# First pass of a fused attention and feed-forward kernel: low weight halves from GpSimd to VectorE, kept bits from GpSimd to ScalarE

## The chip, the cores and the metric

The kernel runs on one core of a Trainium2 chip. The metric is the device time of one execution in microseconds (us), lower is better. Three executions of the kernel before took 726.46, 723.76 and 724.49 us, median 724.49 us. The execution that the profiler recorded took 722.97 us, of which 721.2 us are the span from the first to the last instruction.

## The reference, cut to what matters

```
attn = softmax(causal(q k^T / sqrt(64))) v          # 4 batches, 12 heads, 448 tokens, head size 64
x    = attn as (1792, 768)
xn   = x / sqrt(mean(x^2) + 1e-6) * rms_g
g    = xn @ w_gate                                   # (768, 1536)
out  = (g * sigmoid(g) * (xn @ w_val)) @ w_out       # (1536, 768)
```

q, k, v and rms_g come as 32-bit floats. The three weight matrices come as 64-bit floats and are turned into 32-bit floats on the chip.

## The kernel before, in words

**Splitting.** TensorE multiplies in a rounded 32-bit format (F32R). To keep accuracy each operand is split in two parts, a rounded high part and the rest: `w_h = round(w)`, `w_l = w - w_h` for a weight, `xh`, `xl` for the input and `hh`, `hl` for the hidden layer. Each product is three matmuls: L450 takes `w_h` and `xh`, L451 `w_h` and `xl`, L452 `w_l` and `xh`.

**Passes.** The tokens are worked in three groups: two of 512 and one of 768. The first pass of the feed-forward layer (`s` = 0 to 35, 36 weight tiles of 128x768) works on the first group while the attention of the second group runs between its matmuls; the second pass (`s` = 36 to 71) works on the second group beside the attention of the third; the last part (L600) works on the third group with a fast matrix product. Only the first pass meets the 64-bit weights: it writes each converted tile back to DRAM (`w32`), and the later parts read it from there.

**One weight tile in the first pass.** It is loaded as pairs of 32-bit words (`in_w`, 768 KB, into one of three buffers `w64`). Then:

- `L387`, ScalarE: the high word, read as a 32-bit float, times a power of two into `w_c`.
- `L388`, GpSimd: the high word times zero, so that only its sign is left.
- the kept bits: the top three bits of the low word are put beside that sign. For most tiles this is `L392`, VectorE (shift and or). For the tiles for which `bytes_` holds it is `L390`: the top byte of the low word, times 1/32 less 31/64, is rounded to a 16-bit integer in place. In the text these are the byte tiles. Before, they are the even tiles from 6 on, and L390 is GpSimd's.
- `L394`, VectorE: `w_c` shifted by three, or that word. This ends the use of the `w64` buffer; the load of the tile three later waits for it.
- `L396`: the store to `w32`.
- `L404`, ScalarE: `w_h`. Then `w_l`, on VectorE (`L406`) or on GpSimd (`pool_op`, `L105`).

**What sets the order.** The schedule is manual: the instructions stand on each engine in the order in which the Python code issues them, and every engine works its own queue in that order. Time is counted in ticks, three to a weight tile. `post(d, f)` issues `f` `d` ticks later; the table `T` holds the delays. Tile `s` is converted from five tiles ahead of its matmuls: L387 at once, L388 one tick later, the kept bits four ticks later (`c2`), L394 five ticks later (`c3`) or, for byte tiles, eight (`c38`). `split_w` issues L404 seven ticks ahead of the matmuls and `w_l` two ticks behind it (`wl`; 7 or 5 ticks for the first four tiles). Where two `L394` fall on one tick, they stand next to each other.

**Who empties the banks.** A finished bank of PSUM is read by VectorE: `L467` (`gr`, gate tile) or `L477` (`t_sb`, value tile), in the last tiles `L461`. There are two banks of the name `m_ps`, so the tile after next waits for that read. ScalarE computes the tanh (`L468`), `hh` (`L478`), the exponentials (`L206`) and copies transposed attention weights from PSUM (`L257`, `pt`) for the matmuls `L277`.

All DMAs are issued by SyncE (SP), one queue, in program order.

Of the kernel before, what the change touches and what calls it, by code (L numbers as in the profile page):

```python
# [16 lines left out]
ALU = mybir.AluOpType  # L17
AF = mybir.ActivationFunctionType
# [9 lines left out]
NF = DFF // P  # L28
NU = 2 * NF + 2 * KD
# [11 lines left out]
        for g in range(NG) for c in range(NP)}  # L41
# [2 lines left out]


T = dict(c0=0, c1=1, c2=4, c20=12, c3=5, c30=13, c38=8, c26=6, c36=7, c5=7, c50=16, c56=9, c58=10, exp=1, exp0=3, gt=1, hh=1, hl=4, ws=5, ld2=7,
         ld=4, ld1=11, lv=5, norm0=7, norm1=2, r0=1, r1=5, so=3, wl=2, wl0=7, wl2=5, xl=2, xl0=9)
LOAD = (4, 12, 24, 36, 48, 60, 74, 86)
CONVERT = (20, 32, 44, 56, 62, 93)
SPLIT = (33, 45, 57, 70)  # L50
# [14 lines left out]
def attention_ffn(ctx: ExitStack, tc: tile.TileContext, qk0, qk1, qk2, v, v2, w, g, out, out2):  # L65
# [7 lines left out]
    nc = tc.nc  # L73
# [27 lines left out]
    def f32(ap):  # L101
        return ap.bitcast(F32)

    def pool_op(out_, a, op, b):
        nc.gpsimd.tensor_tensor(out_, a, b, op=op)  # L105
# [27 lines left out]
    def post(delay, fn):  # L133
        if delay <= 0:
            fn()
        else:
            later.setdefault(now[0] + delay, []).append(fn)
# [7 lines left out]
    xr, xh, xl, acc, xq = {}, {}, {}, {}, {}  # L145
# [224 lines left out]
    def convert_ops(s):  # L370
        if s >= NU:
            return []
        raw_w = wt[s]
        t = wr_p.tile([P, DM], F32, tag="w", name="w_c")
        wt[s] = t
        ti, lo, hi = t.bitcast(I32), raw_w[:, :, 0], raw_w[:, :, 1]
        hf_ = raw_w.bitcast(F32)[:, :, 1]
        bytes_ = s > 5 and s % 2 == 0
        if bytes_:
            flat = raw_w.rearrange("p c t -> p (c t)")  # L380
            low = flat.bitcast(I16).rearrange("p (c t) -> p c t", t=4)[:, :, 2]
            top = flat.bitcast(U8).rearrange("p (c t) -> p c t", t=8)[:, :, 3]
        at2, at3, at5 = [T[n] for n in ("c20 c30 c50" if s < 5 else "c26 c36 c56" if s == 5 else
                                        "c2 c38 c58" if bytes_ else "c2 c3 c5").split()]

        return [
            (T["c0"], lambda: nc.scalar.mul(t, hf_, 2.0 ** -112)),  # L387
            (T["c1"], lambda: nc.gpsimd.tensor_scalar(  # L388
                hf_, hf_, 0.0, 1.0, op0=ALU.mult, op1=ALU.mult)),
            (at2, (lambda: nc.gpsimd.tensor_scalar(  # L390
                low, top, 1.0 / 32, -31.0 / 64, op0=ALU.mult, op1=ALU.add)) if bytes_ else
             (lambda: nc.vector.scalar_tensor_tensor(  # L392
                 out=hi, in0=lo, scalar=29, in1=hi, op0=ALU.logical_shift_right, op1=ALU.bitwise_or))),
            (at3, lambda: nc.vector.scalar_tensor_tensor(  # L394
                out=ti, in0=ti, scalar=3, in1=hi, op0=ALU.logical_shift_left, op1=ALU.bitwise_or)),
            (at5, lambda: nc.sync.dma_start(out=w32[s], in_=t)),  # L396
        ]

    def split_w(s):
        if s < 2 * NU:  # L400
            t = wt[s]
            h = ws_p.tile([P, DM], F32R, tag="wh", name="w_h")
            l = ws_p.tile([P, DM], F32R, tag="wl", name="w_l")
            nc.scalar.copy(h, t)  # L404
            if s in (1, 3, 5) or s % 2 == 0 and 4 != s < NU or s > NU + 2 * NF and s % 2:
                post(T[("wl0", "wl0", "wl2", "wl2")[s] if s < 4 else "wl"], lambda: nc.vector.tensor_tensor(l, t, f32(h), op=ALU.subtract))  # L406
            else:
                post(T["wl"], lambda: pool_op(l, t, ALU.subtract, f32(h)))
            wt[s] = tuple(a.rearrange("p (k m) -> p k m", m=P) for a in (h, l))
            u = s - NU  # L410
            if 0 <= u < 2 * NF:
                pair[u % 2] = t
                if u % 2:
                    post(T["ws"], lambda v=u // 2, t0=pair[0], t1=t: quad_sums(v, t0, t1))
# [4 lines left out]
    def quad_sums(v, t0, t1):  # L419

        a11, a12, a21, a22 = t0[:, : HX], t0[:, HX:], t1[:, : HX], t1[:, HX:]
        todo = [(a22, a21, a22, ALU.add), (a21, a11, a21, ALU.subtract),
                (a11, a22, a11, ALU.subtract), (a12, a12, a11, ALU.subtract)]
        for d, (o, x, y, op) in enumerate(todo):
            post(2 * d, lambda o=o, x=x, y=y, op=op: nc.vector.tensor_tensor(o, x, y, op=op))

        def store():
            for d, t in ((wy[v][:, : HX], a11), (wy[v][:, HX:], a22), (wz[v][:, : HX], a21), (wz[v][:, HX:], a12)):
                nc.sync.dma_start(out=d, in_=t)

        post(8, store)
# [383 lines left out]
    with tc.manual_schedule():  # L815
# [28 lines left out]
        for fs, at_ in ((load_w, LOAD), (lambda n: convert(n), CONVERT), (split_w, SPLIT)):  # L844
            for n, t_ in enumerate(at_):
                at_tick(t_, lambda fs=fs, n=n: fs(n))
# [13 lines left out]
        def convert(s):  # L860
            for d, op in convert_ops(s):
                post(d, op)
# [13 lines left out]
        for s in range(2 * NU):  # L876
# [15 lines left out]
            for k0 in (0, 2, 4):  # L892
# [9 lines left out]
                if k0 == (0 if s < 3 else 4) and s + 3 >= len(SPLIT):  # L902
                    split_w(s + 3)
# [129 lines left out]
```

## Time and profile before

| | before |
|---|---|
| median of 3 executions | 724.49 us |
| the profiled execution | 722.97 us |
| its span | 721.2 us |
| TensorE matmul (PE) busy | 683.3 us, 95% |
| VectorE (DVE) busy | 531.7 us, 74% |
| GpSimd (POOL) busy | 393.7 us, 55% |
| ScalarE (ACT) busy | 371.9 us, 52% |
| DMA bytes | 138.80 MB, mean 192 GB/s |

The shares are means over parts that differ: the attention of the first group alone, the first pass, the second pass, and the last part. The rows further below are read by stretches of the span. PEclk, or the granted clock, is the share of TensorE's full clock (2.4 GHz) that the chip granted in a stretch; its other level is half of it. In a row of operations the last part, behind the bar, is the time the engine sat idle just before these instructions and what ended it.

### The profile page before, as it was taken

What the parts mean: (1) busy time and instruction counts of PE and PEld (TensorE: products, weight loads), DVE (VectorE), ACT (ScalarE), POOL (GpSimd) and SP (SyncE); (2) the same over time, 40 slices, a digit from 0 to 9 for tenths busy, and PEclk for the clock granted to TensorE, in tenths of its full rate; (3) what the DMA queues carried; (4) which work ended last, traced back from release to release, by engine and by line L of the source; (5) the groups of instructions that cost most, each with busy time, mean ns of one, the idle gap of its engine ahead of it and who ended that gap; (6) DMA issues with size and microseconds to landing.
All of it is one profiled execution on the core that took longest, in us unless ns stands there. A gap on an engine that the chain in (4) does not pass through costs nothing. (4 is left out here: it accounts for less than half of the span.)

```text
span 721.2 us, 11890 instructions
## 1 busy us (share of the span) xinstructions
PE 683.3 (95%) x4108; PEld 555.8 (77%) x4108; DVE 531.7 (74%) x1017; ACT 371.9 (52%) x832; POOL 393.7 (55%) x324
## 2 busy tenths in 40 slices
PE   8879789988799999999999999999999999999998
PEld 6556567766566667777777777788899999999997
DVE  4997968778667546777768787739567678769993
ACT  6964566855577644534635534433534243355551
POOL 4995498465446763475667656565345354422220
PEclk9999899999799999999999999999999999999999
DMA  8662675845566854657575764533575665643541
GB/s 266 228 233 70 211 261 201 276 167 192 174 223 206 291 196 141 209 185 258 186 265 176 242 204 150 181 105 118 193 232 180 226 220 196 232 137 103 154 143 65
DMA packets 71355, 138.80 MB, mean 192 GB/s; under 512 B 7744, under 2 KB 39232, under 8 KB 71296
## 3 DMA queue, kind: packets, MB, share of 16 engines
q1 hardware_dynamic: 71296, 138.05, 58.1%
q8 instruction: 32, 0.52, 0.3%
q14 instruction: 27, 0.22, 0.1%
HBM read 104.21 MB, written 33.82 MB: 191 GB/s over the span
## 5 line engine op out<-in xcount | busy, mean ns | idle before, releaser
L211 POOL TENSOR_SCALAR sp<-sp,rs 128x384 f32<-128x384 f32 (+3 forms) x132 | 92.2, 716 | 90.9 <-DVE rs L215 76.3
L450 PE MATMUL m_ps<-xh,w_h 128*128 128x512 f32 x276 | 120.6, 437 | 8.9 <-DVE t_sb L477 4.7
L452 PE MATMUL m_ps<-xh,w_l 128*128 128x512 f32 x276 | 111.2, 403 | 2.1 <-POOL w_l L105 2.1
L451 PE MATMUL m_ps<-xl,w_h 128*128 128x512 f32 x276 | 110.6, 401 | 0.0
L206 ACT ACTIVATE sp<-sp,nm 128x384 f32<-128x384 f32 (+3 forms) x168 | 87.2, 523 | 39.7 <-DVE nm L203 39.7
L105 POOL TENSOR_TENSOR a_l<-w_q,a_h 128x768 fp32r<-128x768 f32 x24 | 48.1, 2003 | 65.9 <-ACT a_h L491 65.7
L277 PEld LDWEIGHTS a_ps<-pt,v_r 128*64 128x64 f32 (+1 forms) x864 | 43.8, 138 | 45.3 <-ACT pt L257 14.6
L277 PE MATMUL a_ps<-pt,v_r 128*64 128x128 f32 (+2 forms) x864 | 65.2, 271 | 14.3 <-ACT pt L257 7.5
L450 PEld LDWEIGHTS m_ps<-xh,w_h 128*128 128x128 f32 x276 | 53.6, 194 | 22.9 <-DVE t_sb L477 5.4
L388 POOL TENSOR_SCALAR w<-w 128x768 f32<-128x768 f32 x36 | 42.6, 1184 | 44.0 <-ACT w_c L387 38.1
L452 PEld LDWEIGHTS m_ps<-xh,w_l 128*128 128x128 f32 x276 | 53.2, 193 | 15.1 <-POOL w_l L105 2.9
L105 POOL TENSOR_TENSOR w_l<-w_r,w_h 128x768 fp32r<-128x768 f32 x30 | 59.1, 1976 | 7.4 <-ACT w_h L404 7.3
L451 PEld LDWEIGHTS m_ps<-xl,w_h 128*128 128x128 f32 x276 | 53.9, 195 | 8.3 <-issue 0.2
L203 DVE CUSTOM_DVE_ANT_0 sp<-s_ps,mask 128x128 f32<-128x128 f32 (+3 forms) x136 | 49.7, 414 | 13.9 <-PE s_ps L194 12.8
L255 DVE COPY pt<-t_ps 128x384 f32<-128x384 f32 (+1 forms) x71 | 42.4, 598 | 23.7 <-PE t_ps L251 23.3
L450 PE MATMUL m_ps<-hh,w_h 128*128 128x512 f32 x144 | 58.9, 409 | 0.0
L452 PE MATMUL m_ps<-hh,w_l 128*128 128x512 f32 x144 | 56.6, 393 | 2.0 <-POOL w_l L105 2.0
L451 PE MATMUL m_ps<-hl,w_h 128*128 128x512 f32 x144 | 56.4, 392 | 1.7 <-DVE hl L480 1.7
L387 ACT ACTIVATE w_c<-w 128x768 f32<-128x768 f32 x36 | 32.8, 910 | 39.1 <-DMA w<-in_w 30.8
L394 DVE SCALAR_TENSOR_TENSOR w_c<-w_c,w 128x768 int32<-128x768 int32 x36 | 52.6, 1491 | 0.2
L251 PE MATMUL t_ps<-ident,sp 128*128 128x128 f32 (+1 forms) x309 | 50.6, 276 | 0.4 <-POOL sp L211 0.2
L251 PEld LDWEIGHTS t_ps<-ident,sp 128*128 128x128 f32 (+1 forms) x309 | 38.3, 139 | 15.1 <-POOL sp L211 2.2
(187 smaller groups left out, 1731.2 us busy)
## 6 DMA issues: line engine op xcount, KB each, us to landing
w<-in_w SPq DMA_DIRECT2D x36, 768.0 KB, 5.9
w<-w_c SPq DMA_DIRECT2D x36, 384.0 KB, 6.4
w_r<-w SPq DMA_DIRECT2D x36, 384.0 KB, 4.6
qk_r<-in_qk SPq DMA_DIRECT2D x48, 256.0 KB, 4.4
qk_r<-in_qk SPq DMA_DIRECT2D x12, 512.0 KB, 6.2
v_r<-in_v SPq DMA_DIRECT2D x12, 448.0 KB, 4.8
v_r<-in_v SPq DMA_DIRECT2D x24, 192.0 KB, 3.3
wy<-w_r SPq DMA_DIRECT2D x24, 192.0 KB, 4.4
```

The costliest lines, as they stand in the source:

```text
L105: nc.gpsimd.tensor_tensor(out_, a, b, op=op)
L203: nc.vector.tensor_tensor_reduce(out=sp, in0=ps, in1=mk, scale=nsc, scalar=3.0e38, op0=ALU.add, op1=ALU.min, accum_out=nm)
L206: post(T["exp" if p >= ENDS[0] else "exp0"], lambda: nc.scalar.activation(sp, sp, AF.Exp, bias=nm, scale=-1.0, accum_out=sm))
L211: pr["norms"].append(lambda: nc.gpsimd.tensor_scalar(sp, sp, rs, 1.0, op0=ALU.mult, op1=ALU.mult))
L251: nc.tensor.transpose(ps[:kb, at: at + P], pr["sp"][e][:, o + kb * j: o + kb * (j + 1)], ident)
L255: nc.vector.tensor_copy(pt[:kb, :at], ps[:kb, :at])
L277: nc.tensor.matmul(av_ps[e * D: (e + 1) * D, p % 2, q0: q0 + n], raw_v[p][:kb, h, j, e, :], pr["pt", e][:kb, a0: a0 + n], start=(j == 0), ...
L388: (T["c1"], lambda: nc.gpsimd.tensor_scalar(hf_, hf_, 0.0, 1.0, op0=ALU.mult, op1=ALU.mult)),
L394: (at3, lambda: nc.vector.scalar_tensor_tensor(out=ti, in0=ti, scalar=3, in1=hi, op0=ALU.logical_shift_left, op1=ALU.bitwise_or)),
L450: nc.tensor.matmul(ps, wh[:, k, :], mh, start=(first and k == ks[0]), stop=False)
L451: nc.tensor.matmul(ps, wh[:, k, :], ml, start=False, stop=False)
L452: nc.tensor.matmul(ps, wl[:, k, :], mh, start=False, stop=(last and k == 5))
```

## The change

Four lines change. In the first pass every `w_l` is computed by VectorE; before, sixteen of the 36 were GpSimd's (tile 4 and the odd tiles from 7). The byte tiles are now every third tile from 6 on (6 to 33, ten tiles; before fifteen), and their kept bits are computed by ScalarE with the same arithmetic. So five more tiles take the way through `L392` on VectorE. `w_l` of tile 4 gets the delay 0: it is issued right behind its `w_h`. The second pass keeps its rule.

```diff
-         ... wl=2, wl0=7, wl2=5, xl=2, xl0=9)
+         ... wl=2, wl0=7, wl2=5, wl4=0, xl=2, xl0=9)
...
-        bytes_ = s > 5 and s % 2 == 0
+        bytes_ = s > 5 and s % 3 == 0
...
-            (at2, (lambda: nc.gpsimd.tensor_scalar(
-                low, top, 1.0 / 32, -31.0 / 64, op0=ALU.mult, op1=ALU.add)) if bytes_ else
+            (at2, (lambda: nc.scalar.activation(
+                low, top, AF.Copy, bias=-31.0 / 64, scale=1.0 / 32)) if bytes_ else
...
-            if s in (1, 3, 5) or s % 2 == 0 and 4 != s < NU or s > NU + 2 * NF and s % 2:
-                post(T[("wl0", "wl0", "wl2", "wl2")[s] if s < 4 else "wl"], lambda: nc.vector.tensor_tensor(l, t, f32(h), op=ALU.subtract))
+            if s < NU or s > NU + 2 * NF and s % 2:
+                post(T[("wl0", "wl0", "wl2", "wl2", "wl4")[s] if s < 5 else "wl"], lambda: nc.vector.tensor_tensor(l, t, f32(h), op=ALU.subtract))
```

VectorE early in the first pass, ahead of the `gr` that empties the bank of tile 4 (`w64_970` is the buffer of tile 8, `w_l_1042` belongs to tile 6), as one piece of the difference:

```order
 L469 SCALAR_TENSOR_TENSOR t_sb_1011<-t_sb_1011,gr_1010 128x512
 L477 TENSOR_TENSOR t_sb_1011<-t_sb_1011,x_ps_983 128x512
-L406 TENSOR_TENSOR w_l_1042<-w_c_951,w_h_1041 128x768
-L467 TENSOR_TENSOR gr_1073<-m_ps_1045,rms_924 128x512
+L392 SCALAR_TENSOR_TENSOR w64_970<-w64_970 128x768
+L406 TENSOR_TENSOR w_l_1042<-w_c_952,w_h_1041 128x768
+L394 SCALAR_TENSOR_TENSOR w_c_1005<-w_c_1005,w64_970 128x768
+L467 TENSOR_TENSOR gr_1074<-m_ps_1045,rms_924 128x512
```

Tile 8 is no byte tile any more: its L392 and L394 now stand in front of this `gr`.

VectorE in the middle of the pass, from one `t_sb` (L469) to the next reading of a bank (L477); `w_1843` and `w_1891` are the buffers of tiles 24 and 25. Before:

```order
L469 SCALAR_TENSOR_TENSOR t_sb<-t_sb,gr 128x512
L392 SCALAR_TENSOR_TENSOR w_1891<-w_1891 128x768
L394 SCALAR_TENSOR_TENSOR w_c<-w_c,w_1843 128x768
L394 SCALAR_TENSOR_TENSOR w_c<-w_c,w_1891 128x768
L477 TENSOR_TENSOR t_sb<-t_sb,m_ps 128x512
```

The same place with the change, where the two buffers are called `w_1841` and `w_1893`:

```order
L469 SCALAR_TENSOR_TENSOR t_sb<-t_sb,gr 128x512
L392 SCALAR_TENSOR_TENSOR w_1893<-w_1893 128x768
L406 TENSOR_TENSOR w_l<-w_c,w_h 128x768
L394 SCALAR_TENSOR_TENSOR w_c<-w_c,w_1841 128x768
L394 SCALAR_TENSOR_TENSOR w_c<-w_c,w_1893 128x768
L477 TENSOR_TENSOR t_sb<-t_sb,m_ps 128x512
```

One `w_l` has come in between. GpSimd at the same place, before:

```order
L388 TENSOR_SCALAR w_1843<-w_1843 128x768
L390 TENSOR_SCALAR w_1843<-w_1843 128x768
L388 TENSOR_SCALAR w_1891<-w_1891 128x768
L105 TENSOR_TENSOR acc<-acc,sq 128x512
L105 TENSOR_TENSOR w_l<-w_c,w_h 128x768
L388 TENSOR_SCALAR w_1961<-w_1961 128x768
L390 TENSOR_SCALAR w_1961<-w_1961 128x768
```

and with the change:

```order
L388 TENSOR_SCALAR w_1841<-w_1841 128x768
L388 TENSOR_SCALAR w_1893<-w_1893 128x768
L105 TENSOR_TENSOR acc<-acc,sq 128x512
L388 TENSOR_SCALAR w_1961<-w_1961 128x768
L388 TENSOR_SCALAR w_2012<-w_2012 128x768
```

The two kinds of L390 and `w_l` are gone from it. The L390 of tile 24 stands on ScalarE now, behind the L387 of tile 25 and in front of four exponentials.

## Rows read from the trace of the kernel before

**Rows 1.** Windows: length, busy us (instructions) by engine, granted clock, DMA share, GB/s.

```profile
55.00:262.00 207.00, 184.75 (x865) 134.83 (x865) 150.93 (x248) 126.95 (x291) 129.42 (x85) 0.95 0.61 207
262.00:480.00 218.00, 216.50 (x1648) 162.67 (x1647) 155.14 (x377) 103.43 (x248) 131.01 (x122) 0.99 0.60 195
480.00:721.20 241.20, 236.05 (x1304) 227.90 (x1302) 181.97 (x244) 100.31 (x159) 88.54 (x48) 1.00 0.52 166
```

**Rows 2.** Waits of PE from 55 to 262: us in total, times, longest.

```profile
PE a_ps L277 <- ACT pt L257: 7.5, 7, 1.8
PE m_ps L450 <- DVE t_sb L477: 4.7, 3, 2.7
PE m_ps L450 <- DVE gr L467: 4.1, 1, 4.1
PE m_ps L452 <- POOL w_l L105: 4.0, 4, 1.6
PE m_ps L451 <- DVE hl L480: 1.7, 1, 1.7
```

**Rows 3.** Timeline, PE after one stall: start, us, operation [idle before].

```profile
195.87 0.79 PE L450 MATMUL m_ps<-xh,w_h 128*128 128x512 f32 x1 [1.68 <-DVE t_sb L477]
196.46 0.63 PE L451 MATMUL m_ps<-xl,w_h 128*128 128x512 f32 x1
...
199.58 0.39 PE L451 MATMUL m_ps<-xl,w_h 128*128 128x512 f32 x1
```

**Rows 4.** Operations by shape, 55 to 262: count, busy us, mean ns, idle before.

```profile
L394 DVE SCALAR_TENSOR_TENSOR w_c<-w_c,w 128x768 int32<-128x768 int32 x31 | 44.9, 1482 | 0.0
L388 POOL TENSOR_SCALAR w<-w 128x768 f32<-128x768 f32 x31 | 37.4, 1206 | 44.0 <-ACT w_c L387 38.1 <-PE m_ps L452 3.1 <-DVE xl L331 2.4
L390 POOL TENSOR_SCALAR w<-w 128x768 int16<-128x768 uint8 x15 | 35.2, 2350 | 1.3
L105 POOL TENSOR_TENSOR w_l<-w_c,w_h 128x768 fp32r<-128x768 f32 x16 | 34.6, 2163 | 10.2 <-ACT w_h L404 10.2
L387 ACT ACTIVATE w_c<-w 128x768 f32<-128x768 f32 x31 | 28.1, 906 | 39.1 <-DMA w<-in_w 30.8 <-issue 5.3 <-POOL w_l L105 1.5
...
L392 DVE SCALAR_TENSOR_TENSOR w<-w 128x768 int32<-128x768 int32 x16 | 21.6, 1351 | 8.4 <-POOL w L388 8.4
L406 DVE TENSOR_TENSOR w_l<-w_c,w_h 128x768 fp32r<-128x768 f32 x16 | 19.5, 1216 | 7.1 <-ACT w_h L404 7.1
```

**Rows 5.** Line L394 over the whole span: ns least/median/most.

```profile
L394 DVE SCALAR_TENSOR_TENSOR w_c<-w_c,w x36: 921/1121/2606, 21.2 to 255.2; 128x768 int32<-128x768 int32 x36
```

**Rows 6.** Timeline, VectorE and GpSimd ahead of that stall.

```profile
188.79 2.56 DVE L392 SCALAR_TENSOR_TENSOR w<-w 128x768 int32<-128x768 int32 x1
191.27 3.94 DVE L394 SCALAR_TENSOR_TENSOR w_c<-w_c,w 128x768 int32<-128x768 int32 x2
...
188.66 1.88 POOL L105 TENSOR_TENSOR w_l<-w_c,w_h 128x768 fp32r<-128x768 f32 x1 [0.34 <-ACT w_h L404]
...
192.17 2.49 POOL L390 TENSOR_SCALAR w<-w 128x768 int16<-128x768 uint8 x1
```

**Rows 7.** Timeline, VectorE ahead of PE's longest stall, and later.

```profile
67.29 2.53 DVE L392 SCALAR_TENSOR_TENSOR w<-w 128x768 int32<-128x768 int32 x1
...
80.19 2.12 DVE L469 SCALAR_TENSOR_TENSOR t_sb<-t_sb,gr 128x512 f32<-128x512 f32 x1
...
107.82 0.69 DVE L469 SCALAR_TENSOR_TENSOR t_sb<-t_sb,gr 128x512 f32<-128x512 f32 x1 [1.37 <-ACT t_sb L468]
```

**Rows 8.** Waits, 55 to 262, of ScalarE, GpSimd and SP's queue: total, times, longest.

```profile
ACT w_c L387 <- DMA w<-in_w: 30.8, 15, 3.7
ACT w_h L404 <- DVE w_c L394: 18.1, 7, 4.6
...
POOL w_l L105 <- ACT w_h L404: 10.2, 7, 4.1
...
SPq L362 <- DVE w_c L394: 130.8, 15, 16.7
```

More of the change, by code (lines that the diff above doesn't have):

```diff
@@ L46 @@
 T = dict(c0=0, c1=1, c2=4, c20=12, c3=5, c30=13, c38=8, c26=6, c36=7, c5=7, c50=16, c56=9, c58=10, exp=1, exp0=3, gt=1, hh=1, hl=4, ws=5, ld2=7,
-         ld=4, ld1=11, lv=5, norm0=7, norm1=2, r0=1, r1=5, so=3, wl=2, wl0=7, wl2=5, xl=2, xl0=9)
+         ld=4, ld1=11, lv=5, norm0=7, norm1=2, r0=1, r1=5, so=3, wl=2, wl0=7, wl2=5, wl4=0, xl=2, xl0=9)
 LOAD = (4, 12, 24, 36, 48, 60, 74, 86)
```

## Prediction

> **What bounds the kernel now.** The page's chain of waits comes first and says little here: it reaches back only into the last part, where it is TensorE from end to end. So I read the busy time by stretches. From 262 us on PE is busy 216.50 of 218.00 us and then 236.05 of 241.20 us; in the first pass, 55 to 262 us, it is busy 184.75 of 207.00 us, at a granted clock of 0.95 [rows 1]. The change touches this stretch alone. What it saves there is handed on to the end nearly whole, since PE is full behind it.
>
> In this stretch PE stands idle for 22.25 us. Its waits say for whom: 7.5 us for ScalarE's copies `pt`, 4.7 us and 4.1 us for VectorE to empty a bank, 4.0 us for GpSimd's `w_l`, 1.7 us for `hl` [rows 2]. Behind the longer ones the clock falls: after the 1.68 us wait at 195.87 us a matmul shows 0.63 us, at 199.58 us again 0.39 us [rows 3]; the lower of the two levels is 1.2 GHz. A mean of 0.95 over 207 us is (1 - 0.95) / 0.5 x 207 = 20.7 us at that level. At most 4.1 + 2.7 + 1.7 = 8.5 us of it are the idle times themselves; in the other 12.2 us half is lost, 6.1 us. So 22 + 6 = 28 us is all that the stretch can give.
>
> Why VectorE and ScalarE are late is seen in the durations. VectorE's L394 takes 1482 ns in the mean, L392 of the same shape 1351 ns, `w_l` (L406) 1216 ns [rows 4]; the shortest L394 takes 921 ns [rows 5], which I take as the undisturbed time of all three. The stretch over it is 31 x 0.56 + 16 x 0.43 + 16 x 0.30 = 29 us. The timeline shows what lies beside it: an L392 of 2.56 us and two L394 of 3.94 us while GpSimd works a `w_l` of 1.88 us and kept bits of 2.49 us [rows 6]. VectorE works on when GpSimd's instruction has ended.
>
> **The change part by part.**
>
> *Off GpSimd.* Sixteen `w_l` (34.6 us) and fifteen L390 (35.2 us) go, 69.8 of its 129.42 us [rows 1, 4]. How much of the 29 us goes with them? By share of busy time 54%, 15.7 us; all of it would be 29 us. A wait for a longer instruction is both likelier and longer, so I weigh by number times the square of the mean: 16 x 2.163² + 15 x 2.350² = 158, against 31 x 1.206² = 45 for L388 and at most 29 for the 22 us of shorter ones. That is 68%; I take 20 us.
>
> *On VectorE.* Sixteen `w_l` and five L392 come, 21 x 0.921 = 19.3 us. Its sum hardly changes (150.93 us, +19.3, -20). What changes is where the time lies. For most of these instructions the Trainium skill speaks against the gain (SBUF — State Buffer, Who interferes with whom): a VectorE instruction with two SBUF inputs and a GpSimd instruction that reads SBUF exclude each other, and the later one blocks whole. The rows agree [rows 6]; and by that rule the 21 new ones can be blocked as well, by the L388 that stay. That is the mechanism of my slower rival, priced below from rows.
>
> *On ScalarE.* Ten L390. No row shows this one. From below, L387, the same number of elements at the same stride, takes 906 ns; from above, GpSimd's own form takes 2350 ns [rows 4]. I take 0.91 us, 9.1 us in all, since L387 differs only in the width of its elements; ScalarE then has 136 of 207 us. A free ride (nothing) needs ScalarE to stand idle each time. The skill would have put these on VectorE (ScalarE: Activation LUTs, Rules for kernel authors: plain additions and multiplications belong there). Here L387's 906 ns stand against 921 ns, so nothing is lost in duration; by the rule's placing, VectorE would carry 9.2 us more.
>
> Now the stalls, one kind at a time.
>
> 1. `w_l`, 4.0 us. GpSimd reaches it behind its other work; VectorE gets it two ticks behind `w_h` and takes 0.92 us for 2.16. All four go: -4.0.
> 2. `t_sb`, 4.7 us in three waits. From 188.79 us on L392 and two L394 take 6.42 us [rows 6]. Without `w_l` and L390 they take 3 x 0.92 and once an L388 of 1.21 in the way, 3.97; a new `w_l` of 0.92 stands among them, so 4.9. That is 1.5 us less each time: -0.3, -1.5, -1.5, in all -3.3.
> 3. `gr`, 4.1 us. Ahead of it an L392 takes 2.53 us, and two L469 2.1 us each where 0.69 is to be had [rows 7]: 1.6 + 2 x 1.4 = 4.4 us of stretch, in the timeline beside GpSimd's `w_l` and L390, as in [rows 6]. Added ahead of it are the `w_l` of tile 4 (0.92, which delay 0 puts before the first `gr`) and L392 and L394 of tile 8, 2.8 us together: -1.6, and I take -1.3, since L388 stays.
> 4. `hl`, 1.7 us, behind the same kind of queue: half, -0.9.
> 5. `pt`, 7.5 us, seven waits of about 1.1 us. ScalarE stands behind L404, which waits 18.1 us for L394, and behind L387, which waits 30.8 us for the load of its buffer; and 15 of those loads wait in SP's queue for L394 [rows 8]. L394 a microsecond or so earlier brings both forward. Where every third tile is a byte tile, the loads that a late L394 holds up are those of byte tiles again, whose L394 has three ticks in hand. Bounds: nothing, or all 7.5; I take half, -3.7. Against it stands L390 in front of exponentials or a tanh: ten in 36 tiles, 7 x 10/36 = 2 waits with 0.91 us more, +1.8. Together -2.
> 6. Clock: of the 6.1 us half comes back, as the longest waits shrink without going: -3.
>
> What is late next: a `w_l` in VectorE's queue waits for `w_h`. GpSimd's sixteen waited 10.2 us for it, seven times [rows 8]; on VectorE, L394 and the next reading of a bank stand behind it, and PE waits for that. VectorE is idle a quarter of the time and a bank has a tile's time in hand, so I count a quarter: +2.5.
>
> Sum: -4.0 - 3.3 - 1.3 - 0.9 - 2 - 3 + 2.5 = -12.0 us. Span and surroundings were 722.97 us, so 711; the median of the runs lies 1.5 us above the profiled one, which gives **712 us**. Its own range: if points 3 to 6 give nothing, -4.8, 720; if `hl` and the clock come back whole and L390 costs nothing, -17.6, 707.
>
> **Rivals.**
>
> *Nearly all stalls go.* If the even spread of loads frees ScalarE, every kind goes but 4 us (half of `gr`, a few `pt`): 28 - 4 = 24 us, 700 us. For it: VectorE and ScalarE each have a quarter and more of the stretch to spare. Against it: in-order queues with more in them, and a first stall which the order rows fill again.
>
> *No net change.* ScalarE's waits for loads (30.8 us) set the pace, and the loads are no smaller. Then only point 1 is won, and L390 (+1.8) and the wait for `w_h` (+2.5) take it back: 724 us. Against it: loads wait for L394 fifteen times, not for the DMA engines, which are busy 0.61 [rows 1].
>
> *Slower: the exchange only moves the block into VectorE's queue.* Each moved `w_l` costs 0.92 us and its share of the wait, 10.2 / 16 = 0.64 us, in front of a bank's reading: 16 x 1.56 = 25 us. Against it count 4.0 us of point 1 and 3 x 2.4 us of shorter L392 and L394: 13.8 us remain, and if half finds no idle time it costs 7 us: 731 us. It decides from where a pair of tiles adds more to the queue (3.1 us) than the lock gives back. A kept-bits instruction of 2.35 us on ScalarE would do the same: 10 x 1.44 = 14 us more in front of the tanh.
>
> **How the numbers follow.** Forecast 0.56, nearly all 0.19, no change 0.13, slower 0.12. About 0.5% (3.6 us) is what a measurement of this kernel can tell from no change. Faster is the first two, 0.75; same 0.13; slower 0.12. The range reaches to 702, past which half of the second case lies, and to 727, past which most of the fourth lies.
>
> **What the changed profile would show.** Right: in the first pass no wait of PE for POOL; L394 and L392 with means near 1.1 us; GpSimd near 60 us there, VectorE near 150, ScalarE near 136; L390 on ScalarE near 0.9 us; waits for `t_sb` under 1.5 us in all; a granted clock of 0.97 or more; everything behind the pass as before, only earlier. Wrong: PE waiting for L452 with DVE `w_l` as the releaser; L406 idle for `w_h` by more than 15 us; `pt` waits above 7.5 us; L394 still near 1.5 us, which would say that L388 or something else held the lock.

## The result and the profile after

The changed kernel took 715.09 us (median of 4 runs, 714.10 to 716.26), the kernel before 724.12 us beside it (4 runs, 723.67 to 726.46): a ratio of 0.9869, 95% interval 0.9841 to 0.9898, or 9.0 us less. The forecast was 712 us in a range of 702 to 727. The profiled execution took 715.93 us with a span of 714.1 us, 7.1 us less than before.

The first pass ended earlier, and what it saved was carried to the end: the first `gr` of the second pass stands at 286.36 us before and at 279.79 us after, 6.6 us earlier. So 55 to 262 us before answers to 55 to 255.4 us after. Window of the changed kernel, with the columns of [rows 1]:

```profile
55.00:255.40 200.40, 181.89 (x860) 135.12 (x857) 143.33 (x268) 144.17 (x301) 54.87 (x54) 0.94 0.62 212
```

PE's idle time in the stretch is 200.40 - 181.89 = 18.51 us, where it was 22.25. That is 3.7 of the 6.6 us. The other 2.9 us show as less busy time at a clock that is no higher (0.94 for 0.95), with 860 for 865 recorded matmuls; the trace doesn't split them further. GpSimd is down to 54.87 us, VectorE to 143.33 us; ScalarE is up to 144.17 us.

Waits of PE from 55 to 258 us, with the columns of [rows 2]:

```profile
PE a_ps L277 <- ACT pt L257: 13.1, 8, 3.2
PE m_ps L450 <- DVE gr L467: 5.0, 2, 3.3
PE m_ps L450 <- DVE t_sb L477: 0.3, 1, 0.3
```

Three of the five kinds of [rows 2] are gone or all but gone: `w_l` (4.0 us), `hl` (1.7) and `t_sb` (4.7 to 0.3). These three rows are all that is left. `gr` is a little longer (4.1 to 5.0 us), and `pt` has nearly doubled, from 7.5 to 13.1 us. Operations by shape, 55 to 255 us, with the columns of [rows 4]:

```profile
L394 DVE SCALAR_TENSOR_TENSOR w_c<-w_c,w 128x768 int32<-128x768 int32 x31 | 33.5, 1103 | 0.0
L406 DVE TENSOR_TENSOR w_l<-w_c,w_h 128x768 fp32r<-128x768 f32 x31 | 31.8, 1027 | 12.5 <-ACT w_h L404 12.4
L387 ACT ACTIVATE w_c<-w 128x768 f32<-128x768 f32 x31 | 28.2, 909 | 25.7 <-DMA w<-in_w 25.7
L392 DVE SCALAR_TENSOR_TENSOR w<-w 128x768 int32<-128x768 int32 x21 | 20.0, 952 | 5.7 <-POOL w L388 5.6
L390 ACT ACTIVATE w<-w 128x768 int16<-128x768 uint8 x10 | 19.5, 1948 | 0.1
```

VectorE's instructions lost their stretch as forecast: L394 from 1482 to 1103 ns, L392 from 1351 to 952, L406 from 1216 to 1027 [rows 4]. The Trainium skill's rule that a VectorE instruction with two SBUF inputs and a GpSimd instruction that reads SBUF exclude each other (SBUF — State Buffer, Who interferes with whom) agrees with that; below it is called the lock. But L390 on ScalarE takes 1948 ns, not the 910 that I took. The waits behind it, 55 to 258 us, against [rows 8]:

```profile
ACT w_c L387 <- DMA w<-in_w: 25.7, 12, 4.0
...
DVE w_l L406 <- ACT w_h L404: 12.4, 7, 4.4
...
ACT w_h L404 <- DVE w_c L394: 8.5, 4, 2.6
...
SPq L362 <- DVE w_c L394: 103.0, 10, 13.9
```

Ten loads wait for L394 where fifteen did, and ScalarE still stands 25.7 us at L387 for its load. One such place shows how it reaches PE. Timeline of the changed kernel (start, us, operation [idle before]):

```profile
188.22 1.81 DVE L394 SCALAR_TENSOR_TENSOR w_c<-w_c,w 128x768 int32<-128x768 int32 x2
189.23 0.33 SPq L362 DMA_DIRECT2D w<-in_w  x1
...
195.25 0.91 ACT L387 ACTIVATE w_c<-w 128x768 f32<-128x768 f32 x1 [3.96 <-DMA w<-in_w]
...
199.81 0.61 ACT L468 ACTIVATE t_sb<-gr 128x512 f32<-128x512 f32 x1
...
201.04 0.47 ACT L257 COPY pt<-t_ps 128x384 f32<-128x384 f32 x1
...
201.56 0.65 PE L277 MATMUL a_ps<-pt,v_r 128*64 128x256 f32 x2 [2.20 <-ACT pt L257]
202.22 1.92 ACT L390 ACTIVATE w<-w 128x768 int16<-128x768 uint8 x1
...
203.87 0.59 ACT L257 COPY pt<-x_ps 128x384 f32<-128x384 f32 x1
...
204.51 1.54 PE L277 MATMUL a_ps<-pt,v_r 128*64 128x256 f32 x6 [2.30 <-ACT pt L257]
```

Read it downwards. Two L394 stand next to each other; the first frees a `w64` buffer, and the load that wants it goes out at 189.23 us. It lands six microseconds later; ScalarE has stood 3.96 us at the L387 of that tile, with exponentials, a tanh and the copy `pt` queued behind it. PE waits 2.20 us for that `pt`. Then L390 stands in front of the next one, and PE waits 2.30 us again.

The other new wait is for `gr`. Timeline of the changed kernel around PE's longest stall, which begins with a late load and an L390:

```profile
86.07 0.90 ACT L387 ACTIVATE w_c<-w 128x768 f32<-128x768 f32 x1 [2.37 <-DMA w<-in_w]
...
86.88 1.95 ACT L390 ACTIVATE w<-w 128x768 int16<-128x768 uint8 x1
...
90.61 0.82 ACT L404 CAST w_h<-w_c 128x768 fp32r<-128x768 f32 x1
...
91.46 0.96 DVE L406 TENSOR_TENSOR w_l<-w_c,w_h 128x768 fp32r<-128x768 f32 x1 [2.02 <-ACT w_h L404]
...
92.34 2.48 DVE L394 SCALAR_TENSOR_TENSOR w_c<-w_c,w 128x768 int32<-128x768 int32 x2
...
94.74 0.68 DVE L467 TENSOR_TENSOR gr<-m_ps,rms 128x512 f32<-128x512 f32 x1
...
95.57 0.47 PE L450 MATMUL m_ps<-xh,w_h 128*128 128x512 f32 x1 [3.29 <-DVE gr L467]
```

ScalarE waits 2.37 us at L387 for its load, then works L390, and both delay `w_h`; VectorE stands 2.02 us at the `w_l` that needs it, with two L394 and the `gr` behind; PE stands 3.29 us. That is the wait that the prediction named as late next.

### The profile page after: what moved, and what is told of

Its sections match the earlier page's. It is cut to its first block, busy times and chain, and to the rows that moved or that the text cites. A ratio compares the mean times of both kernels' runs of the same rounds, so it can differ in the third digit from the quotient of the medians.

```text
span 714.1 us, 11892 instructions
## 1 busy us (share of the span) xinstructions
PE 680.7 (95%) x4108; PEld 555.8 (78%) x4108; DVE 525.1 (74%) x1038; ACT 389.0 (54%) x842; POOL 318.4 (45%) x293
## 5 line engine op out<-in xcount | busy, mean ns | idle before, releaser
L211 POOL TENSOR_SCALAR sp<-sp,rs 128x384 f32<-128x384 f32 (+3 forms) x132 | 90.2, 701 | 102.4 <-DVE rs L215 86.9
L388 POOL TENSOR_SCALAR w<-w 128x768 f32<-128x768 f32 x36 | 39.4, 1096 | 105.0 <-ACT w_c L387 96.9
L277 PE MATMUL a_ps<-pt,v_r 128*64 128x128 f32 (+2 forms) x864 | 64.8, 272 | 19.5 <-ACT pt L257 13.1
L450 PEld LDWEIGHTS m_ps<-xh,w_h 128*128 128x128 f32 x276 | 53.1, 192 | 19.3 <-issue 10.5
L387 ACT ACTIVATE w_c<-w 128x768 f32<-128x768 f32 x36 | 32.9, 913 | 25.7 <-DMA w<-in_w 25.7
L406 DVE TENSOR_TENSOR w_l<-w_c,w_h 128x768 fp32r<-128x768 f32 x36 | 36.6, 1016 | 12.5 <-ACT w_h L404 12.4
```

What stands on the lines that cost most here:

```text
L211: pr["norms"].append(lambda: nc.gpsimd.tensor_scalar(sp, sp, rs, 1.0, op0=ALU.mult, op1=ALU.mult))
L277: nc.tensor.matmul(av_ps[e * D: (e + 1) * D, p % 2, q0: q0 + n], raw_v[p][:kb, h, j, e, :], pr["pt", e][:kb, a0: a0 + n], start=(j == 0), ...
L388: (T["c1"], lambda: nc.gpsimd.tensor_scalar(hf_, hf_, 0.0, 1.0, op0=ALU.mult, op1=ALU.mult)),
L450: nc.tensor.matmul(ps, wh[:, k, :], mh, start=(first and k == ks[0]), stop=False)
```

## The experiments

The two parts of the change were taken apart, and two suspects were taken away one at a time: the delay of the byte tiles' L394 (`c38`, eight ticks; the others have five) and the instruction L390. Diffs are against the changed kernel where nothing else is said. Each kernel ran beside the kernel before on the same chip (medians 722.72, 722.13 and 722.26 us), so kernels of different chips are compared by their ratios; 0.1% is 0.72 us, and a difference of two ratios is uncertain by 0.2 to 0.4%.

| label | `w_l` of the first pass | byte tiles, L390 | their L394 | us | ratio, 95% interval |
|---|---|---|---|---|---|
| before | split | 15, GpSimd | +8 | 724.12 | 1 |
| after | VectorE | 10, ScalarE | +8 | 715.09 | 0.9869 (0.9841 to 0.9898) |
| e2_wl_only | VectorE | 15, GpSimd | +8 | 724.89 | 1.0021 (1.0003 to 1.0039) |
| e7_bits_only | split | 10, ScalarE | +8 | 719.04 | 0.9959 (0.9944 to 0.9975) |
| e3_bits_pool | VectorE | 10, GpSimd | +8 | 706.93 | 0.9784 (0.9759 to 0.9810) |
| e5_none_late | VectorE | none | +8 in 10 tiles | 704.76 | 0.9752 (0.9724 to 0.9779) |
| e8_before_early | split | 15, GpSimd | +6 | 707.16 | 0.9788 (0.9762 to 0.9814) |
| e10_before_none | split | none | +5 | 705.38 | 0.9765 (0.9741 to 0.9790) |
| e9_wl_early | VectorE | 15, GpSimd | +6 | 699.95 | 0.9690 (0.9663 to 0.9717) |
| e4_bits_none | VectorE | none | +5 | 695.04 | 0.9616 (0.9592 to 0.9639) |
| e6_bits_early | VectorE | 10, ScalarE | +6 | 694.95 | 0.9615 (0.9589 to 0.9641) |

**e1_probe: why L390 takes 1.95 us.** A kernel of its own that times single instructions, each form three times, one behind the other; its lines for L390's form and, below, with dense operands:

```
nc.scalar.activation(dst["i16s"], src["u8s"], AF.Copy, bias=-31.0 / 64, scale=1.0 / 32)
nc.scalar.activation(dst["i16d"], src["u8d"], AF.Copy, bias=-31.0 / 64, scale=1.0 / 32)
```

> Computes nothing of the reference: it only times single instructions on 128x768 elements, three of each, one behind the other, and writes zeros. In the changed kernel the kept bits on ScalarE take 1948 ns, where the forecast had 0.91. Theory A (narrow strided target): writing 16-bit elements eight bytes apart costs it; then u8 strided to int16 strided and f32 dense to int16 strided (L88, L95) take about 1.9 us, u8 strided to f32 dense (L89) about 0.9. Theory B (narrow source): reading bytes eight bytes apart costs it; then L88, L89 and L94 take about 1.9, and L90, L95 about 0.9. Theory C (narrow types, dense or not): L91 takes about 1.9 as well. For the same form VectorE (L98) is open: 0.9 us if it runs at one element a cycle, near 0.5 if it runs at two.

It took 72.35 us. Operations by line, ns least/median/most. L88 is L390's form (bytes eight apart to 16-bit words eight bytes apart), L94 has a dense target, L91 both operands dense; L95 goes from dense 32-bit floats to the strided 16-bit target; L96 is GpSimd and L98 VectorE in L390's form, L97 and L99 the same with both dense:

```profile
L88 ACT ACTIVATE t<-raw x3: 1899/1900/1901, 6.2 to 10.1; 128x768 int16<-128x768 uint8 x3
...
L91 ACT ACTIVATE t<-raw x3: 842/843/843, 20.6 to 22.3; 128x768 int16<-128x768 uint8 x3
...
L94 ACT ACTIVATE t<-raw x3: 880/881/882, 28.6 to 30.4; 128x768 int16<-128x768 uint8 x3
L95 ACT ACTIVATE t<-f x3: 1903/1904/1904, 31.3 to 35.2; 128x768 int16<-128x768 f32 x3
L96 POOL TENSOR_SCALAR t<-raw x3: 1886/1887/1888, 37.2 to 41.1; 128x768 int16<-128x768 uint8 x3
L97 POOL TENSOR_SCALAR t<-raw x3: 831/831/832, 43.1 to 44.9; 128x768 int16<-128x768 uint8 x3
L98 DVE TENSOR_SCALAR t<-raw x3: 1017/1017/1018, 45.8 to 47.9; 128x768 int16<-128x768 uint8 x3
L99 DVE TENSOR_SCALAR t<-raw x3: 559/560/560, 48.9 to 50.1; 128x768 int16<-128x768 uint8 x3
```

The source costs next to nothing (843 to 881 ns, L91 and L94), the target a factor of 2.2 (881 to 1900, L94 and L88), whatever is read (L95). L387, by which I had priced L390, reads at that stride but writes a dense target. GpSimd pays the same, 1887 ns, which is most of the 2350 ns that its L390 took. The stride alone does not do it on GpSimd: L388 writes 32-bit words at the same stride, and the kernel before shows (ns least/median/most)

```profile
L388 POOL TENSOR_SCALAR w<-w x36: 875/1011/1673, 15.7 to 252.4; 128x768 f32<-128x768 f32 x36
```

or 875 ns at the least, beside 831 with both operands dense (L97). For ScalarE no 32-bit target at that stride was timed.

**e2_wl_only: the first half alone.** All `w_l` on VectorE, tile 4's early; the kept bits as before, on GpSimd for every even tile from 6 on.

```diff
-        bytes_ = s > 5 and s % 3 == 0
+        bytes_ = s > 5 and s % 2 == 0
-            (at2, (lambda: nc.scalar.activation(low, top, AF.Copy, bias=-31.0 / 64, scale=1.0 / 32)) if bytes_ else
+            (at2, (lambda: nc.gpsimd.tensor_scalar(low, top, 1.0 / 32, -31.0 / 64, op0=ALU.mult, op1=ALU.add)) if bytes_ else
```

> The change's first half alone: every w_l of the first pass on VectorE, kept bits of the even tiles still on GpSimd. Lock theory (the gain is GpSimd's long instructions gone from beside VectorE's): about half of the stretched time stays, since the fifteen kept-bits instructions of 2.35 us stay and now meet sixteen more w_l; no PE wait for w_l; 719 us, between 716 and 722. Rival (the gain is only the 4.0 us in which PE waited for GpSimd's w_l): the whole gain of those waits is here, 720, and the second half gives nothing by itself. Rival (VectorE's queue): without the second half it is no faster than before, 724.

Measured: 724.89 us, ratio 1.0021. That is slower than the 716 to 722 us of the lock theory. The half on which the prediction built most of its gain gives nothing alone. Its time is the third case's (724), but not by its reason: PE waits for VectorE 8.5 us (`t_sb` 4.9, `gr` 2.1, `hl` 1.5), where [rows 2] have 10.5. Waits, 55 to 250 us:

```profile
ACT w_c L387 <- DMA w<-in_w: 41.5, 17, 5.3
PE a_ps L277 <- ACT pt L257: 10.0, 9, 1.8
```

PE no longer waits for `w_l`, L406 and L392 are shorter (1123 and 998 ns), and in place of what they free stands a longer wait of ScalarE for its loads, 41.5 us where [rows 8] have 30.8.

**e3_bits_pool: L390 back on GpSimd, ten tiles.**

```diff
-            (at2, (lambda: nc.scalar.activation(low, top, AF.Copy, bias=-31.0 / 64, scale=1.0 / 32)) if bytes_ else
+            (at2, (lambda: nc.gpsimd.tensor_scalar(low, top, 1.0 / 32, -31.0 / 64, op0=ALU.mult, op1=ALU.add)) if bytes_ else
```

> The change with the kept bits of its ten byte tiles back on GpSimd. Toll theory (the ten L390 of 1.95 us on ScalarE stand in front of pt copies, tanh and w_h and make PE wait 13.1 us for pt instead of 7.5): pt waits fall to 6 to 8 us; but the lock comes back for ten instructions of 2.35 us, with L394 and L406 means from 1.1 to about 1.25 us; the two nearly cancel, 715, between 712 and 718. Rival (pt waits come from the loads, which ScalarE waits for 25.7 us): pt waits stay at 11 us or more and the lock is added, 718 to 720.

Measured: 706.93 us, ratio 0.9784, 0.85% below the changed kernel and below the bounds of both theories. So putting the kept bits on ScalarE made the change worse, not better. PE's `pt` waits fall from 13.1 to 7.7 us. Against e2, which differs only in fifteen byte tiles for ten, it is 2.37% faster: that is where the change's gain comes from.

**e4_bits_none: no byte tiles.** Every tile takes L392, and every L394 its five ticks.

```diff
-        bytes_ = s > 5 and s % 3 == 0
+        bytes_ = False
```

> The change without byte tiles: the kept bits of all 36 tiles on VectorE as L392, none on ScalarE or GpSimd. Ten L392 of 0.95 us come to VectorE, 19.5 us go from ScalarE, and all L394 stand five ticks behind the conversion, so no load waits for a late L394. Toll theory: pt waits fall below 6 us, VectorE near 152 us in the stretch, 711, between 707 and 714. Rival (VectorE's queue bounds now): gr and t_sb waits of PE grow beyond 8 us, 717 or more. Rival (loads): 715 unchanged.

Measured: 695.04 us, ratio 0.9616. VectorE has ten instructions more and the kernel is 2.5% faster than the changed one; every theory had it at 707 us or more. Waits, 55 to 250 us:

```profile
PE m_ps L450 <- DVE gr L467: 3.5, 1, 3.5
...
ACT w_c L387 <- DMA w<-in_w: 3.1, 1, 3.1
...
PE a_ps L277 <- ACT pt L257: 1.9, 1, 1.9
...
SPq L362 <- DVE w_c L394: 14.0, 1, 14.0
```

**e5_none_late: the late L394 without L390.** As e4, but L394 and the store of every third tile at 8 and 10 ticks.

```diff
-        bytes_ = s > 5 and s % 3 == 0
+        bytes_ = False
+        late = s > 5 and s % 3 == 0
-                                        "c2 c38 c58" if bytes_ else "c2 c3 c5").split()]
+                                        "c2 c38 c58" if late else "c2 c3 c5").split()]
```

> As the run without byte tiles (695 us), all kept bits on VectorE, but for every third tile from 6 on L394 and the store again at eight and ten ticks instead of five and seven, as byte tiles have them. Load theory (a late L394 holds the buffer, the load of the tile three later starts late, ScalarE's L387 waits for it and all behind it): about ten loads are held again, ScalarE waits 20 us or more for in_w, 704, between 700 and 708. Rival (the byte instructions themselves, 1.95 us on ScalarE or 2.2 us on GpSimd, cost the time): unchanged, 694 to 697.

Measured: 704.76 us, ratio 0.9752, 1.36% above e4 though not one instruction differs, only when ten L394 and their stores are issued. Waits, 55 to 250 us (line numbers are one higher here):

```profile
ACT w_c L388 <- DMA w<-in_w: 30.4, 14, 4.0
...
ACT w_h L405 <- DVE w_c L395: 8.4, 4, 2.7
...
PE a_ps L277 <- ACT pt L257: 7.4, 8, 2.2
...
SPq L362 <- DVE w_c L395: 85.8, 9, 13.9
```

The wait for the load and the `pt` waits are back with nothing but the delay, and in SP's queue the loads now wait for L394 (85.8 us, 14.0 in e4). The delay also puts pairs of L394 side by side in VectorE's queue. That is not what costs: PE's waits for VectorE (`gr` and `t_sb`) are 4.0 us here and 4.3 us in e4. But a late L394 also reaches ScalarE directly: `w_h` waits for it, 8.4 us here and 1.8 in e4. The runs don't separate this from the load; the wait for the load grows by 27.3 us, this one by 6.6.

**e6_bits_early: the changed kernel with the delay shortened.**

```diff
- ... c38=8, ... c58=10 ...
+ ... c38=6, ... c58=8 ...
```

> The changed kernel with one thing moved: L394 and the store of its byte tiles at six and eight ticks instead of eight and ten, so that no load is issued ahead of the L394 that frees its buffer. L390 stays on ScalarE, 1.95 us, ten times. Load theory: ScalarE's waits for in_w fall below 10 us, 703, between 698 and 708. Toll theory (L390 in front of pt copies and tanh is what costs): 712 to 716, pt waits stay above 10 us.

Measured: 694.95 us, ratio 0.9615, the same as with no byte tiles and 3 us below the load theory's bounds. L390 is still on ScalarE, and as long:

```profile
L390 ACT ACTIVATE w<-w 128x768 int16<-128x768 uint8 x10 | 19.5, 1948 | 0.6 <-POOL w L388 0.6
```

Waits, 55 to 250 us:

```profile
DVE w_c L394 <- ACT w L390: 11.9, 8, 3.1
...
PE a_ps L277 <- ACT pt L257: 3.3, 2, 2.9
PE m_ps L450 <- DVE gr L467: 2.9, 1, 2.9
ACT w_c L387 <- DMA w<-in_w: 2.0, 3, 1.1
```

Loads still wait for L394 in SP's queue (49.2 us, nine times), but they land in time for L387. With that, 19.5 us of L390 on ScalarE, in place of ten L392 on VectorE, cost nothing that shows (against e4); with late loads they cost 1.17% (changed kernel against e5). VectorE even waits 11.9 us for them, off the path.

**e7_bits_only: the second half alone.** Ten byte tiles with L390 on ScalarE; `w_l` split as before.

```diff
-            if s < NU or s > NU + 2 * NF and s % 2:
+            if s in (1, 3, 5) or s % 2 == 0 and 4 != s < NU or s > NU + 2 * NF and s % 2:
```

> The change's second half alone: kept bits of every third tile on ScalarE, w_l as before (sixteen on GpSimd). Load theory: ten held loads instead of fifteen, most of the change's gain is here, 714 to 718, though PE waits for GpSimd's w_l by 2 to 4 us remain. Lock theory (the w_l on GpSimd are VectorE's main hindrance): 721 or more.

Measured: 719.04 us, ratio 0.9959, between the bounds of the two theories. Half a percent alone; with it in place, moving `w_l` is worth 0.90%, where in e2 it was worth nothing.

**e8_before_early: the kernel before with the delay shortened,** by the same diff as e6.

> The kernel before with one thing moved: L394 and the store of its fifteen byte tiles at six and eight ticks instead of eight and ten. Sixteen w_l and fifteen kept-bits instructions stay on GpSimd. Load theory: held loads go, ScalarE's waits for in_w fall from 30.8 us to below 12, 708, between 702 and 714. Lock theory: the long GpSimd instructions still block VectorE, 720 to 726.

Measured: 707.16 us, ratio 0.9788. Two numbers in a table give the kernel before more than the whole change did. Waits of PE, 55 to 250 us:

```profile
PE m_ps L452 <- POOL w_l L105: 4.2, 3, 2.2
PE m_ps L450 <- DVE gr L467: 4.1, 1, 4.1
PE m_ps L450 <- DVE t_sb L477: 3.9, 5, 2.4
...
PE a_ps L277 <- ACT pt L257: 0.9, 2, 0.6
```

`pt` is gone from 7.5 us [rows 2]; `w_l`, `gr` and `t_sb` stand as before.

**e9_wl_early and e10_before_none: what moving `w_l` is worth with the loads on time.** e9 is e2 with `c38=6, c58=8`, and differs from e8 in `w_l` alone; e10 is the kernel before with `bytes_ = False`, and differs from e4 in `w_l` alone.

> All w_l on VectorE, the fifteen even byte tiles with L390 on GpSimd, their L394 at six ticks in place of eight. The only difference to e8_before_early (707.2 us) is where w_l is computed. Theory A (moving w_l gives nothing while loads are held, but once the loads are on time it is what bounds the pass): PE waits for GpSimd's w_l (4.2 us in e8) and t_sb (3.9 us) go, 698 to 701 us. Theory B (moving w_l is worth nothing at all; L394 and L392 are stretched by L390 on GpSimd as well): 707 us, within 2 us of e8.

> The kernel before with no byte tile at all: w_l split between VectorE and GpSimd as before, kept bits on VectorE for every tile. Together with e4_bits_none (w_l on VectorE, no byte tiles, 695.0 us) it shows again what moving w_l is worth with the loads on time. Theory A (moving w_l is worth several us with the loads on time): 700 to 704 us, with PE waiting for GpSimd's w_l about 4 us. Theory B (the held loads were all): 695 us, within 2 us of e4.

Measured: 699.95 us (0.9690) and 705.38 us (0.9765). Moving `w_l` is worth 0.98% with early byte tiles (e8 to e9) and 1.49% with none (e10 to e4), 7 to 11 us. Theory A holds in both; e10 came out 1.4 us above its bounds. Waits of PE in e9, 55 to 250 us:

```profile
PE m_ps L450 <- DVE t_sb L477: 4.8, 5, 1.3
PE m_ps L450 <- DVE gr L467: 3.6, 1, 3.6
```

Against e8 the 4.2 us for GpSimd's `w_l` are gone (3.7 us in e10, none in e4). `t_sb` isn't: L390 is still on GpSimd there, and L406 (1264 ns) and L394 (1173 ns) are still long.

**e11_wl4_two: the fifth tile.**

```diff
- ... wl4=0 ...
+ ... wl4=2 ...
```

> The changed kernel, but w_l of the fifth tile with the usual delay of two ticks. Theory A (the delay 0 changes only the early wait for gr, 1.73 us at 82 us or 3.29 us at 95 us): 713 to 717 us. Theory B (w_l of the fifth tile two ticks later makes the matmuls of tile 4 wait for it and hands that on): 717 to 720 us, with a wait of L452 for DVE w_l.

Measured: 713.81 us, ratio 0.9885 (0.9859 to 0.9911), the same as the changed kernel within the intervals. PE shows 4.5 us of waits for `gr` (5.0 in the changed kernel) and none for `w_l`. That part of the change decides nothing.

A fourth `w64` buffer, which might take the hold away without moving L394 and so part the two ways in which a late L394 reaches ScalarE, was not tried.

## Why the prediction was right, and where its reasons were not

**The place was right, and the time in part by luck.** The gain lies in the first pass, is handed on whole, and comes out at 9.0 us for 12. But of the 9.0 us of idle time in the sum (12.0 less 3 for the clock) only 3.7 came; 2.9 us more are shorter busy time that the trace doesn't explain. And the step that won, fewer loads held, has no term of its own in the sum.

**The bound of 28 us was too low.** e4 and e6 take 27.8 us (3.85% of 722) out of the stretch, and PE is still idle 6.4 us of what is left. Window of e6, with the columns of [rows 1]:

```profile
55.00:235.00 180.00, 173.64 (x871) 130.31 (x872) 142.85 (x270) 143.91 (x301) 58.03 (x56) 0.99 0.70 237
```

PE's busy time fell by 11.1 us (184.75 to 173.64), where the bound counted 6.1 us for the clock.

**Points 1, 2 and 4 came true, and more so.** `w_l` 4.0 to none, as forecast; `t_sb` 4.7 to 0.3, where 1.4 was to be left; `hl` 1.7 to none, where half was. Together -10.1 us for a forecast of -8.2.

**Point 3 (`gr`, -1.3) failed.** 4.1 us became 5.0. The stall that I had worked out shrank from 4.1 us to 1.73 (at 82.18 us), better than forecast, but the one at 95.57 us, shown above, came new. It takes L390 and the late L394 together: at that place PE waits 0.79 us with late L394 and no L390 (e5), 1.00 us with L390 on GpSimd (e3), and not at all with L390 on ScalarE and L394 two ticks earlier (e6). (The fifth tile's delay has no part in it that shows, e11.)

**Point 5 (`pt`, -2) has the wrong sign, and is where most of the lost microseconds are:** +5.6 us; `pt` waits above 7.5 us were one of the prediction's own signs of being wrong. Two things failed in it. The mis-sized term is L390: 0.91 us was taken, 1.95 measured, near the upper bound of 2.35; ten of them are 19.5 us instead of 9.1, and with late loads they cost 0.85% against leaving them on GpSimd (e3), about 6 us. The fear that I filed under the slower rival (2.35 us on ScalarE cost 14 us) was the better guide. The other is the sentence that the loads held up are those of byte tiles again, "whose L394 has three ticks in hand". L394 has. But the instruction that waits for the load is L387, and ScalarE's queue is in order: exponentials, tanh and `pt` stand behind it, and they have nothing in hand. Nor are the late loads those of byte tiles alone: the next tile's load goes out only behind the held one, as at 225.21 and 227.89 us, and ScalarE waits for both (3.43 us at 231.12 us, 1.72 us at 237.65 us).

**Point 6 (clock, -3) gave nothing,** and the 0.97 named as a sign of being right did not come: (1 - 0.94) / 0.5 x 200.4 = 24.0 us at the lower level, 20.7 before. The waits that remained are as long as those that went: 3.29 us at 95.57 us, 3.16 us at 162.88 us.

**"Late next" was right.** L406 waits 12.4 us for `w_h`, near the 10.2 taken over from GpSimd and below the 15 that I set as the mark; it shows in the `gr` stall.

**The cause was weighted wrongly.** The sum made GpSimd's lock the main term. Step by step the runs say: `w_l` to VectorE +0.21% (e2), fifteen byte tiles to ten -2.37% (e2 to e3), L390 from GpSimd to ScalarE +0.85% (e3 to after); together -1.31%. The middle step, which I counted as five more L392, is the whole gain: each byte tile whose L394 comes at eight ticks holds a buffer, and with it a load. That this is the late L394 and not L390 is shown by e5 (the delay alone costs 1.36%) and e6 (L390 alone costs nothing that shows); fifteen L390 on GpSimd with the loads on time cost 0.74% (e4 to e9), so by an estimate the five that e3 drops explain about 0.25% of the 2.37. The stretch of VectorE's instructions was real. Moving `w_l` is worth 7 to 11 us with the loads on time and 0.90% (6.5 us) with ten of them held (e7 to after); while fifteen were held it was worth nothing. How much of the 7 to 11 us is the lock is not shown: about 4 us are PE's own waits for GpSimd's `w_l` (4.2 in e8, 3.7 in e10).

**The rivals.** "Nearly all stalls go" has nearly the price that e4 and e6 reached (700 us for 695) and names the right lever, the spread of loads; it takes the delay as well to get there. "No net change" argued that ScalarE's waits for loads set the pace, which is what the runs show; I argued against it that the loads wait for L394 and not for the DMA engines. That was true and was no argument against: a load held by L394 stops ScalarE just as well.

**The better version.** By the ratios, e4 and e6 are both about 18 us faster than the changed kernel (2.5%) and 28 us faster than the one before.

## What to carry to other kernels

When an engine waits for a load, look at what holds the load's buffer before counting bytes: here last readers issued two or three ticks late, with time in hand themselves, cost 10 to 24 us (1.36%, e4 to e5, to 3.31%, e9 to e2) through an in-order queue on another engine. Stalls taken off one chain can be worth nothing while another ends last, as in e2, so price a change's parts both with that chain in place and with it gone. An instruction's duration is taken over from one with the same source and the same target, not from one with the same element count.

## What the runs showed that was not expected

A 16-bit target eight bytes apart costs 1900 ns for 128x768 on ScalarE, 1887 on GpSimd and 1017 on VectorE, against 843, 831 and 560 with both operands dense; a source at that stride costs ScalarE 881 for 843 (e1). The Trainium skill's advice to leave plain multiplications and additions to VectorE (ScalarE: Activation LUTs, Rules for kernel authors) fits this form better than I granted it: 1017 against 1900 ns. And the same 19.5 us of it cost about 8 us or nothing, by whether the loads beside it were late (after against e5, e6 against e4).
